# Two attention blocks backward: another order of the steps, an earlier last pair and refill at the block boundary, and x^T of the second block by a transposing DMA

## The chip, the cores and the metric

One core of one Trainium2 chip (the groups of runs were on different chips). The metric is the device time of one execution in microseconds, the median of several; every comparison below is with runs of the kernel before that were taken in the same rounds on the same chip. All runs used are in the fast state; the granted TensorE clock of the profiled ones is 0.993 to 0.998.

## The reference

Forward and gradients of two independent attention blocks with cached K and V. For each block B = 8 batches of 96 queries, D = 640, H = 32 heads of 128, 512 keys, all bf16:

```python
def _A_ref(x, k_cache, v_cache, wq, wo):
    q = (x @ wq).reshape(B, Sq, H, Dh).transpose(0, 2, 1, 3)
    scores = jnp.einsum("bhqd,bhkd->bhqk", q, k_cache) * (Dh ** -0.5)
    p = softmax(scores)
    o = jnp.einsum("bhqk,bhkd->bhqd", p, v_cache)
    return o.transpose(0, 2, 1, 3).reshape(B, Sq, H * Dh) @ wo
# out = concatenate([A, B], -1); outputs: out and, by vjp with grad_out,
# dx, dk, dv, dwq, dwo of both blocks
```

## The kernel before

The kernel is one list of pieces of work sorted by (tick, slot) and emitted in that order. A tick, called **step** here, is one head and one batch, so a block has 256 steps and heads go in pairs (16 steps for a pair). Steps are counted below from the start of block 2: step 0 is its first, negative ones belong to block 1. Each piece has an offset from the start of its pair (`HK`) or of its step (`OFF`); within a step `SLOTS` gives the order. All DMAs are issued by one queue, the sync engine's, in that same order.

```python
OFF = dict(kt=-3, vt=2, vn=1, kn=4, dv=7, dk=10, s2=3, s3=3, s4=4, s5=5, s6=6, s7=8, s8=9)
HK = [   # first and second head of a pair: loads, wo^T/wq^T, Q, dO, their transposes, O and dQ back, dwo, dwq
    dict(pA=-10, pB=-7, pC0=[-6, -4], pC1=[-5, -3], pD1=-2, pD0=0, qA0=21, qA1=25, qB=[28, 25]),
    dict(pA=-7, pB=-2, pC0=[-1, 1], pC1=[0, 2], pD1=3, pD0=6, qA0=29, qA1=33, qB=[36, 33], qD=[...]),
]
HK2 = [dict(HK[0], qA0=29, qB=[32, 31]), dict(HK[1], qA0=33)]      # first pair of block 2
GT0, ST0, ST1, NG0, NX0 = 2, -14, 7, 21, 26
SLOTS = dict(LOAD=0, S2A=5, S2B=5.5, S8=10, S7=20, S5=30, S4=40, S6=50, ...)
# S2: S and softmax; S8: dQ, dS^T; S7: dK; S5: O, P^T; S4: dV; S6: dP, delta, dS

# boundary, block 2: x and g are staged in three "ob" buffers and transposed on TensorE
for i in range(2 * TT):
    em.add(tick0 + ST0 + (ST1 * i) // (2 * TT), SL_LOAD + 0.5, setup_stage(i // TT, i % TT))
    em.add(tick0 + ST0 + (ST1 * i) // (2 * TT) + 2, SL_SETUP, setup_T(i // TT, i % TT))
for t in range(TT):    # refill of the single g_nat and x_nat, which the last pair of block 1 still reads
    em.add(tick0 + NG0 + t, SL_LOAD + 0.5, setup_nat(1, t, t + 1))
    em.add(tick0 + NX0 + (3 * t) // 2, SL_LOAD + 0.5, setup_nat(0, t, t + 1))
# ...
def qB(h, di):         # dwo of one head, in two pieces (columns 0:512 and 512:640)
    if "dwo_sb" not in st:
        st["dwo_sb"] = hd.tile([128, D], BF16, name="dwo_sb", bufs=1)
    # ... 6 matmuls into w_ps, then evac() by ScalarE into dwo_sb
# ...
for di in range(len(dsplits)):
    em.add(c0t + hk["qB"][min(di, len(hk["qB"]) - 1)], SL_HEAD + 1, qB(h, di))
em.add(c0t + max(hk["qB"]) + 2, SL_LOAD + 0.3, qB_st(h))      # the store, two steps later
```

Other single or scarce buffers that matter: `dK_sb` has three, `V_sb`, `K_sb` and `VT_p` four, `KT_p` five, and all PSUM tiles share eight banks. A second `dwo_sb` takes 1.25 KB more in each partition of SBUF; the experiments pay for it with a `KT_p` buffer, as the author found no room otherwise (no run here shows that).

## Time and profile before

| | before |
|---|---|
| median of 4 runs | 1669.48 us (1669.2 to 1673.67) |
| profiled span, granted clock | 1668.0 us, 0.993 |
| busy: TensorE, VectorE, ScalarE, GpSimd | 97%, 82%, 80%, 32% |
| TensorE busy in a slice of 41.7 us: steady / at the boundary | 41.4 to 41.7 in most (three of block 1: 38.6, 40.5, 40.9) / 31.6 to 41.1 |

Read the slices, not the average: a steady slice of TensorE is full, so only what takes columns off its stream or fills its few holes can change the time. The prediction shows the lines.

### The profile page before, as it was taken

To read this page: it belongs to the slowest core of one execution; us is meant where nothing else is said; L and a number is where in the kernel's file an instruction comes from. 1 tells how busy PE (TensorE), PEld (TensorE's weight loads), DVE (VectorE), ACT (ScalarE), POOL (GpSimd) and SP (SyncE) were. 2 spreads that over 40 slices of the span, in tenths; PEclk is the share of its full clock that TensorE was granted. 3 is DMA by queue.
4 is the path that set the end of the run, shared out by engine and by line. 5 is a ranking of instruction groups with operands and counts; after the bars stand their busy time and mean duration, and the time that the engine had idled before them with its cause. 6 is when DMAs were issued, how large, how long until landed. Compare 5 with 4: busy or idle time off the path is not lost.

```text
span 1668.0 us, 55517 instructions
## 1 busy us (share of the span) xinstructions
PE 1616.8 (97%) x20920; PEld 1265.7 (76%) x20920; DVE 1368.3 (82%) x3389; ACT 1339.2 (80%) x3517; POOL 533.5 (32%) x1030
## 2 busy tenths in 40 slices
PE   7999999999999999998998799999999999999998
PEld 5777877777777777877777678777787777878776
DVE  5887888888888888887887678888888888888886
ACT  6989877779788788886877699778797887878783
POOL 2333333333333333332333233333333333333331
PEclk9999999999999999999999899999999999999999
DMA  9999999999999999999999999999999999999995
GB/s 253 265 280 270 279 283 270 267 282 273 291 271 287 278 280 279 298 257 271 274 295 282 284 252 281 289 279 267 282 297 286 275 266 276 288 273 270 281 281 173
DMA packets 372430, 458.13 MB, mean 275 GB/s; under 512 B 36800, under 2 KB 363968, under 8 KB 363968
## 3 DMA queue, kind: packets, MB, share of 16 engines
q1 hardware_dynamic: 372160, 454.57, 102.7%
q8 instruction: 164, 2.69, 0.7%
q14 instruction: 106, 0.87, 0.1%
HBM read 161.09 MB, written 159.12 MB: 192 GB/s over the span
## 4 chain that ended last, share of the span: by engine, by line
PE 79%; ACT 6%; DMA 6%; DVE 5%; issue 2%; SPq 1%; POOL 0%; ACTq 0%; DVEq 0%
PE q_ps L239 11%; PE o_ps L524 10%; PE dwo_ps L479 6%; PE dV_ps L375 5%; PE dP_ps L399 5%; PE dwq_ps L499 5%; PE S_ps L303 5%; PE dK_ps L441 5%; PE optp_ps L350 4%; PE optp_ps L357 4%; PE dq_dst_ps L418 4%; PE dq_dst_ps L425 4%; PE n_ps L254 3%; PE nat_ps L465 2%; DVE negm L305 2%
## 5 line engine op out<-in xcount | busy, mean ns | idle before, releaser
L334 POOL TENSOR_SCALAR P_sb<-E_sb,rinv 96x512 bf16<-96x512 bf16 x512 | 352.7, 689 | 297.4 <-DVE rinv L325 296.8
L389 POOL TENSOR_TENSOR prod<-OT_h,dOT_h 128x96 bf16<-128x96 bf16 x512 | 186.8, 365 | 806.0 <-DVE OT_h L361 757.6
L446 ACT ACTIVATE dK_sb<-dK_ps 128x512 bf16<-128x512 f32 x512 | 304.4, 594 | 166.2 <-PE dK_ps L441 159.9
L315 ACT ACTIVATE E_sb<-S_ps,negm 96x512 bf16<-96x512 f32 x512 | 349.4, 682 | 74.3 <-DVE negm L305 68.8
L403 DVE SCALAR_TENSOR_TENSOR dS_sb<-dP_ps,dl_ps,P_sb 96x512 bf16<-96x512 f32 x512 | 382.4, 747 | 24.4 <-PE dl_ps L401 13.6
L305 DVE TENSOR_REDUCE negm<-S_ps 96x1 f32<-96x512 f32 x512 | 346.8, 677 | 57.1 <-PE S_ps L303 56.5
L380 ACT ACTIVATE dV_sb<-dV_ps 128x512 bf16<-128x512 f32 x512 | 309.7, 605 | 0.3 <-PE dV_ps L375 0.3
L364 ACT ACTIVATE PT_sb<-optp_ps 128x384 bf16<-128x384 bf16 x512 | 252.7, 493 | 5.0 <-DVE OT_h L361 4.2
L375 PE MATMUL dV_ps<-dOnat_h,P_sb 96*128 96x128 bf16 x2048 | 199.2, 220 | 0.0
L441 PE MATMUL dK_ps<-Qnat_h,dS_sb 96*128 96x128 bf16 x2048 | 198.6, 220 | 0.0
L427 DVE COPY dST_sb<-dq_dst_ps 128x384 bf16<-128x384 bf16 x512 | 177.6, 347 | 25.0 <-PE dq_dst_ps L425 20.2
L399 PE MATMUL dP_ps<-VT_p,dOT_h 128*96 128x512 bf16 x512 | 196.2, 383 | 0.0
L303 PE MATMUL S_ps<-KT_p,QT_h 128*96 128x512 bf16 x512 | 194.7, 380 | 1.5 <-ACT E_sb L315 0.4
L350 PE MATMUL optp_ps<-PT_sb,V_sb 128*128 128x96 bf16 x2048 | 172.4, 206 | 18.7 <-ACT dwo_sb L162 9.8
L357 PE MATMUL optp_ps<-ident,P_sb 96*128 96x96 bf16 x2048 | 172.6, 206 | 4.9 <-POOL P_sb L334 4.4
L418 PE MATMUL dq_dst_ps<-dST_sb,K_sb 128*128 128x96 bf16 x2048 | 171.4, 207 | 1.4 <-DVE dST_sb L427 1.1
L418 PEld LDWEIGHTS <-K_sb 128*128 128x128 bf16 x2048 | 133.3, 98 | 51.3 <-issue 2.9
L425 PE MATMUL dq_dst_ps<-ident,dS_sb 96*128 96x96 bf16 x2048 | 172.1, 205 | 0.0
L361 DVE CAST OT_h<-optp_ps 128x96 bf16<-128x96 f32 x512 | 126.6, 247 | 49.2 <-PE optp_ps L357 44.7
L524 PE MATMUL o_ps<-wo_r,OT_h 128*128 128x512 bf16 (+1 forms) x768 | 149.3, 299 | 0.0
L524 PE MATMUL o_ps<-wqT_h,dQT_h 128*128 128x512 bf16 (+1 forms) x768 | 148.5, 299 | 0.0
L350 PEld LDWEIGHTS <-V_sb 128*128 128x128 bf16 x2048 | 125.2, 97 | 23.0 <-issue 18.2
(71 smaller groups left out, 3064.4 us busy)
## 6 DMA issues: line engine op xcount, KB each, us to landing
out_dram<-dV_sb SPq DMA_DIRECT2D x256, 256.0 KB, 4.7
out_dram<-dK_sb SPq DMA_DIRECT2D x256, 256.0 KB, 4.6
V_sb<-in_A_v_cache_dram SPq DMA_DIRECT2D x128, 256.0 KB, 4.4
K_sb<-in_A_k_cache_dram SPq DMA_DIRECT2D x128, 256.0 KB, 4.5
V_sb<-in_B_v_cache_dram SPq DMA_DIRECT2D x128, 256.0 KB, 4.5
K_sb<-in_B_k_cache_dram SPq DMA_DIRECT2D x128, 256.0 KB, 4.4
out_dram<-dwo_sb SPq DMA_DIRECT2D x64, 160.0 KB, 4.6
out_dram<-dwq_sb SPq DMA_DIRECT2D x32, 320.0 KB, 4.7
```

The lines of the kernel that those rows point to most:

```text
L305: nc.vector.tensor_reduce(negm[:], S_ps[:], axis=AX.X, op=ALU.max, negate=True)
L315: nc.scalar.activation(E_sb[:].rearrange("q (a f) -> q a f", f=F4), st["S_ps"][:].rearrange("q (f a) -> q a f", f=F4), ACT.Exp, bias=st["n ...
L334: nc.gpsimd.tensor_scalar(P_sb[:], st["E_sb"][:], st["rinv"][:], 0.0, op0=ALU.mult, op1=ALU.add)
L350: nc.tensor.matmul(OT_ps, st["V_sb"][:, c, :], st["PT_sb"][:, c * Sq:(c + 1) * Sq], start=(c == 0), stop=(c == KC - 1))
L375: nc.tensor.matmul(dV_ps[:, c * 128:(c + 1) * 128], P_sb[:, c * 128:(c + 1) * 128], hs["dOnat_h"][:, b * 128:(b + 1) * 128], start=True, s ...
L380: nc.scalar.activation(dV_p[:, j], dV_ps[:], ACT.Identity, scale=1.0)
L399: nc.tensor.matmul(dP_ps[:], hs["dOT_h"][:, tok], st["VT"], start=True, stop=True)
L403: nc.vector.scalar_tensor_tensor(dS_sb[:].rearrange("q (a f) -> q a f", f=F4), dP_ps[:].rearrange("q (f a) -> q a f", f=F4), dl_ps[:, 0:1] ...
L418: nc.tensor.matmul(dQT_ps, st["K_sb"][:, c, :], st["dST_sb"][:, c * Sq:(c + 1) * Sq], start=(c == 0), stop=(c == KC - 1))
L441: nc.tensor.matmul(dK_ps[:, c * 128:(c + 1) * 128], dS_sb[:, c * 128:(c + 1) * 128], hs["Qnat_h"][:, b * 128:(b + 1) * 128], start=True, s ...
L446: nc.scalar.activation(dK_p[:, j], dK_ps[:], ACT.Identity, scale=1.0)
L524: nc.tensor.matmul(o_ps[:], src[:, t * 128:(t + 1) * 128], rhs, start=(hh == 0), stop=(hh == groups[g] - 1))
```

## The change

Its intent, part by part: **(a)** x^T of block 2 comes by five transposing DMAs instead of thirty TensorE transposes, g is staged four steps ahead, and the heads of block 2's first pair move with it; **(b)** the last pair of block 1 does its dwo and dwq sooner (`HKE`), so that the refills of g and x can start at step 15 and spread to step 28, and block 2's first pair does its dwo sooner; **(c)** wq and wo are loaded two steps sooner; **(d)** at the start g and the first wo are loaded two steps sooner; **(e)** inside a step TensorE does dK, dQ and dS^T, dP, O and P^T, dV. The diff, cut to its core:

```diff
-    dict(pA=-10, pB=-7, ...),
+    dict(pA=-12, pB=-7, ...),
-HK2 = [dict(HK[0], qA0=29, qB=[32, 31]), dict(HK[1], qA0=33)]
-GT0, ST0, ST1, NG0, NX0 = 2, -14, 7, 21, 26
+HK2 = [dict(HK[0], pB=-5, pC0=[-6, -4], pC1=[-1, 0], pD1=1, pD0=2, qB=[28, 27]), dict(HK[1], pC0=[-2, 0], pC1=[1, 2])]
+HKE = [dict(HK[0], qB=[23, 22]), dict(HK[1], qA0=25, qA1=27, qB=[29, 28], qD=[(30, 0, 2), (31, 2, 4), (32, 4, 5)])]
+GT0, NG0, NX0 = 0, 15, 18
-SLOTS = dict(..., S8=10, S7=20, S5=30, S4=40, S6=50, ...)
+SLOTS = dict(..., S7=10, S8=20, S6=25, S5=30, S4=40, ...)
+            sp(nc.sync.dma_start_transpose(S["xT"][:, c, :], x_flat[:, c * 128:(c + 1) * 128]))
-        for i in range(2 * TT):    # staging and TensorE transposes of x and g
-            ...
+        for c in range(DC):
+            em.add(tick0 - 14 + c, SL_LOAD + 0.5, setup_xT(c))
+        for t in range(TT):
+            tt = tick0 - 8 + 5 * (t // 3)
+            em.add(tt - 4, SL_LOAD + 0.5, setup_stage(t))
+            em.add(tt, SL_HEAD - 1, setup_T(1, t))
-            em.add(tick0 + NX0 + (3 * t) // 2, SL_LOAD + 0.5, setup_nat(0, t, t + 1))
+            em.add(tick0 + NX0 + 2 * t, SL_LOAD + 0.6, setup_nat(0, t, t + 1))
-            hk = (HK if h >= HP else HK1 if first else HK2)[j]
+            hk = (HKE if first and h >= H - HP else HK if h >= HP else HK1 if first else HK2)[j]
+            soon = 2 if first and HP <= h < 2 * HP and j == 0 else 0    # pair 1 keeps its load steps
```

More of the change, by code (lines that the diff above doesn't have):

```diff
@@ L46 @@
 HK = [
-    dict(pA=-10, pB=-7, pC0=[-6, -4], pC1=[-5, -3], pD1=-2, pD0=0, qA0=21, qA1=25, qB=[28, 25]),
+    dict(pA=-12, pB=-7, pC0=[-6, -4], pC1=[-5, -3], pD1=-2, pD0=0, qA0=21, qA1=25, qB=[28, 25]),
     dict(pA=-7, pB=-2, pC0=[-1, 1], pC1=[0, 2], pD1=3, pD0=6, qA0=29, qA1=33, qB=[36, 33], qD=[(37, 0, 2), (38, 2, 4), (39, 4, 5)]),
@@ L57 @@
 GSPREAD1 = 9
-SLOTS = dict(LOAD=0, S2A=5, S2B=5.5, S8=10, S7=20, S5=30, S4=40, S6=50, S3A=52, S3B=53, S5B=54, HEAD=SL_HEAD, GRP=SL_GRP)
+SLOTS = dict(LOAD=0, S2A=5, S2B=5.5, S7=10, S8=20, S6=25, S5=30, S4=40, S3A=52, S3B=53, S5B=54, HEAD=SL_HEAD, GRP=SL_GRP)
 class Chain:
@@ L134, in setup_nat, with setup_stage, setup_xT, f @@
         return f
-    def setup_stage(which_, t):
+    def setup_stage(t):
         def f():
-            key, _, src_flat = KEYS[which_]
-            S[(key, t)] = wk.tile([128, D], BF16, name="ob", bufs=3)
-            sp(nc.sync.dma_start(S[(key, t)][:], src_flat[t * 128:(t + 1) * 128, :]))
+            S[("g_nat", t)] = wk.tile([128, D], BF16, name="ob", bufs=3)
+            sp(nc.sync.dma_start(S[("g_nat", t)][:], g_flat[t * 128:(t + 1) * 128, :]))
+        return f
+    def setup_xT(c):
+        def f():
+            if c == 0:
+                S["xT"] = const.tile([128, DC, T], BF16, name="xT", bufs=1)
+            sp(nc.sync.dma_start_transpose(S["xT"][:, c, :], x_flat[:, c * 128:(c + 1) * 128]))
         return f
@@ L176, in build_block @@
     else:
-        for i in range(2 * TT):
-            em.add(tick0 + ST0 + (ST1 * i) // (2 * TT), SL_LOAD + 0.5, setup_stage(i // TT, i % TT))
-            em.add(tick0 + ST0 + (ST1 * i) // (2 * TT) + 2, SL_SETUP, setup_T(i // TT, i % TT))
+        for c in range(DC):
[4 more added lines that the diff above has]
+            em.add(tt, SL_HEAD - 1, setup_T(1, t))
         for t in range(TT):
             em.add(tick0 + NG0 + t, SL_LOAD + 0.5, setup_nat(1, t, t + 1))
-            em.add(tick0 + NX0 + (3 * t) // 2, SL_LOAD + 0.5, setup_nat(0, t, t + 1))
+            em.add(tick0 + NX0 + 2 * t, SL_LOAD + 0.6, setup_nat(0, t, t + 1))
     def pA_wq(h):
@@ L551, in build_block @@
             c0t = tick0 + (h - j) * B
-            hk = (HK if h >= HP else HK1 if first else HK2)[j]
+            hk = (HKE if first and h >= H - HP else HK if h >= HP else HK1 if first else HK2)[j]
             early = first and h < HP
+            soon = 2 if first and HP <= h < 2 * HP and j == 0 else 0
             if j == 0:
-                em.add(tick0 - 15 if early else c0t + hk["pA"], SL_LOAD + (1 if early else 0), pA_wq(h))
-            em.add(tick0 + GT0 if early else c0t + hk["pA"], SL_LOAD - 1 if early else SL_LOAD, pA(h))
+                em.add(tick0 - 15 if early else c0t + hk["pA"] + soon, SL_LOAD + (1 if early else 0), pA_wq(h))
+            em.add(tick0 + GT0 if early else c0t + hk["pA"] + soon, SL_LOAD - 1 if early else SL_LOAD, pA(h))
             em.add(c0t + hk["pB"], SL_HEAD, pB(h))
```

## The prediction

> **What bounds the kernel now.** I read first the page's busy shares, then the stretches table (the span in 40 equal slices, busy time of each engine), then the table of waits, then the timeline around the largest waits. The page:
>
> ```profile
> PE 1616.8 (97%) x20920; PEld 1265.7 (76%) x20920; DVE 1368.3 (82%) x3389; ACT 1339.2 (80%) x3517; POOL 533.5 (32%) x1030
> PE 79%; ACT 6%; DMA 6%; DVE 5%; issue 2%; SPq 1%; POOL 0%; ACTq 0%; DVEq 0%
> ```
>
> TensorE is busy 97% and is 79% of the chain that ended last. A busy TensorE need not run at its rate, so I checked in the timeline that it streams: from the first dP matmul of a step to the next instruction there are 0.22 us for 512 columns, and four 128-column dK matmuls take 0.22 to 0.23 us. Away from the ends and the block boundary the slices look like the first row below; only a few do not (columns: PE, PEld, DVE, ACT, POOL busy us with counts, granted clock, DMA share, GB/s).
>
> ```profile
> 417.00:458.70 41.70, 41.55 (x524) 31.86 (x523) 34.93 (x88) 32.12 (x84) 12.51 (x25) 1.00 1.05 291
> 750.60:792.30 41.70, 37.09 (x470) 29.40 (x468) 30.14 (x75) 27.52 (x70) 10.62 (x21) 0.96 1.00 271
> 834.00:875.70 41.70, 40.16 (x507) 30.35 (x506) 33.55 (x87) 32.66 (x88) 12.87 (x25) 1.00 1.07 295
> 875.70:917.40 41.70, 37.33 (x470) 29.24 (x469) 32.18 (x81) 30.70 (x81) 12.94 (x25) 0.96 1.03 282
> 917.40:959.10 41.70, 31.56 (x405) 25.40 (x402) 25.11 (x60) 25.53 (x70) 9.94 (x20) 0.88 1.02 284
> ```
>
> So the steady state is bound by the TensorE stream itself and the idle time sits in 750 to 960 us, where block 1 hands over to block 2 (plus 14 us in the first two slices and 5 in the last). What TensorE waits for there, from the table of its waits:
>
> ```profile
> PE optp_ps L350 <- ACT dwo_sb L162: 9.8, 1, 9.8
> PE woT_ps L209 <- DMA wo_r<-in_A_wo_dram: 4.8, 4, 2.2
> PE optp_ps L350 <- DMA V_sb<-in_B_v_cache_dram: 4.2, 2, 2.6
> PE tp_ps L151 <- DMA ob<-in_grad_out_dram: 3.3, 2, 2.8
> PE tp_ps L151 <- DMA ob<-in_B_x_dram: 1.8, 2, 1.5
> ```
>
> The 9.8 us is one wait. ScalarE's timeline shows it: nothing runs on it from 927.7 to 937.8, as it stands at the write of dwo_sb of head 1 (second row) behind the store of head 0 out of the same single buffer.
>
> ```profile
> 927.25 0.49 ACT L364 ACTIVATE PT_sb<-optp_ps 128x384 bf16<-128x384 bf16 x1
> 937.79 0.28 ACT L162 ACTIVATE dwo_sb<-dwo_ps 128x128 bf16<-128x128 f32 x1 [10.05 <-DMA out_dram<-dwo_sb]
> ```
>
> The sync queue's timeline says why the store was late: it issues at 933.31 and lands at 937.7, and the queue had been issuing back to back since 906 because the x and g refills stood in it among the K and V loads:
>
> ```profile
> 926.59 0.46 SPq L133 DMA_DIRECT2D x_nat<-in_B_x_dram  x1
> 927.10 1.23 SPq L266 DMA_TRANSPOSE KT_p<-in_B_k_cache_dram  x1
> 929.95 0.47 SPq L133 DMA_DIRECT2D x_nat<-in_B_x_dram  x1
> 933.31 0.46 SPq L485 DMA_DIRECT2D out_dram<-dwo_sb  x1
> ```
>
> **What the Trainium skill says.** "TensorE: Matmul & The Clock Gate", section "Wait — 56ns, not 53.3ns?", gives columns over 2.4 GHz plus about 2.5 ns from start to start; the 0.22 us for 512 columns and for 4 x 128 columns agree. The same page, section "Part 1: The HAM clock gate", has the clock halve after an idle window of about 3.4 us; the slice with the 9.8 us wait has a granted clock of 0.88, the other two with waits 0.96, so it agrees, and a wait costs more than its length. The same page, "Architectural detail: the array is 16x 32x32, not 1x 128x128", calls ScalarE and VectorE strict FIFO; the empty ScalarE above agrees. "DMA: Bandwidth & Descriptors", section "DMA Transpose (X-bar)", allows transposing DMAs only from the sync and scalar queues, of 2-byte data, into SBUF; x is bf16 and all transposes stay on one queue, so no wait between streams is added. KT_p already comes this way (5.1 us to landing).
>
> **The change, part by part.** A step (the code's tick) is one head and batch: S_ps matmuls start 3.15 us apart on average. Per two steps the sync queue issues two transposing loads (1.1 to 1.2 us each), two plain loads (0.53), two stores (0.42), with about 0.1 between: near 4.7 of 6.3 us. So 1.6 us in two steps is left, room for three extra DMAs at 0.52.
>
> (a) x^T of block 2 by DMA. Gone: 30 transposes on TensorE, 30 x 0.056 = 1.7 us of stream, and 6 evictions off ScalarE and VectorE. g^T stays on TensorE but is staged four steps ahead, not two (12 us against a landing of 4.4), so the waits on "ob" (3.3 + 1.8) and the issue waits of the third staging buffer go. The slice at 750 lost 41.55 - 37.09 = 4.5 us of busy time and 0.04 x 41.7 = 1.7 us of clock, the next one 0.4: 6.6 us, all of it gone if the queue keeps up. Sum -8.3. Against: in steps -14 to -7 before block 2 the queue gets 5 transposes, 6 stagings and 6 of the usual extras, by my count 30.5 us against 25 of TensorE work; the loads run four steps ahead, less landing some 4 us of slack, so the excess of 5 costs about +1.5. Net -7.
>
> (b) The last pair of block 1 and the refills. The new qB order of block 2's first pair stores head 0 at step 30 and rewrites at 33; before, the rewrite (33) stood ahead of the store (34). That removes the 9.8 us for certain. The three slices from 834 lost 1.4 + 4.2 + 10.0 = 15.6 us of busy time; of their clock loss (1.7 + 5.0) about 3 lies outside the waits: 18.5 in all. But refills are not thinner, only earlier: g at 15 to 20, x at 18 to 28 (before 21 to 26 and 26 to 33), beside the twelve output stores at 8 to 26. With dwo and dwq moved ahead, steps 20 to 25 carry little TensorE work (about 2.4 us each by adding up their matmuls), and there I count 19.7 us of queue against 14.5. Summing from step 18 the queue falls some 7 us behind; before, the same count gave 5 and the waits on V_sb (4.2). With 4 us of slack I keep +4. Net -14.5.
>
> (c) wq, wo two steps earlier from pair 2 on: the late wo_r in the steady state, 1.1 us. Pair 1 keeps its time, so its wait (2.2) stays. Net -1.
>
> (d) g loads at step 0, not 2, with the first wo: one of the woT waits, 1.5 us, less a little for V later in the queue. Net -1.
>
> (e) Step order. No instruction is added. dK first gives dST one more 0.22 us before dQ reads it; dP before O gives P_sb 0.25 us more before P^T and starts VectorE's dS earlier. dl comes 0.55 us sooner after S, so prod has less time. All engines have the same work, and the steady slices have at most 0.2 us of visible idleness each, so it can earn only the rest: "optp_ps <- P_sb" 4.4 us (half at the two ends), "dwo_ps <- dK_sb" 2.4, 0.3 at the shortest step of each second pair. I take -3.
>
> Sum: -7 - 14.5 - 1 - 1 - 3 = -26.5, so 1669.7 - 26.5 = 1643 us, 1.6% less.
>
> **The rivals.** First, the queue lag replaces the wait (the likeliest). For it: the DMA share is 1.0 and over everywhere, landings come back to back from 885 to 937, and the light steps 20 to 25 lie exactly in the new refill. It would put V_sb waits of 8 to 10 us there and 3 to 5 at -8, where a wait over 3 us also halves the clock: 1652 to 1656. Against it: while TensorE waits the queue catches up, so loss cannot exceed its lag of 7. Second, the order creates a wait of its own: P_sb (0.69) and prod (0.37) share GpSimd, and in steps under 2.3 us (4 of 32) dl may stand waiting for prod, 0.3 us each: 512/32 x 4 x 0.3 = 19 us at worst, ending near 1662. Against it: GpSimd is 32% busy and from the end of O the chain of copy, dS and prod comes to about 1.6 us, under the shortest step of 1.8. Third, the order does more than I grant: S, dP and dV are spread more evenly over the eight banks, so head matmuls meet freed banks and the small gaps after dl and n_ps also go; with no lag at the boundary that is 1669.7 - 8.3 - 18.5 - 2 - 8 = 1633. Fourth, the transpose of x in 256-byte rows is much slower than that of KT and holds the queue; each 5 us of that shows as a wait on xT before q_ps, up to +10. No row of the profile has such a shape.
>
> **Range and chances.** The sure part is 9.8 + 5.1 + 1.7 = 16.6 us, giving 1653; the full sum of everything found is 1633. With order and lag each uncertain by some 6 us I say 1643, with 1630 to 1657. Over 2% faster means below 1636.3: that needs the third rival without the first, 0.23. Slower by 2% would need the order to cost 60 us: 0.01. Within 2%: 0.76.
>
> **What would show it.** Right: no tp_ps wait and no tp_ps matmul on x in block 2; no ScalarE gap on dwo_sb over 1 us; slices from 750 to 960 at 40 us busy or more and clock 1.00, except one near steps 20 to 26 with V_sb or VT_p waits of a few us; steady slices at 41.5. Wrong: TensorE waits for V_sb summing above 8 us (first rival), a dl_ps wait on prod recurring in every pair (second), TensorE idle under 20 us in all with the span below 1635 (third), q_ps waiting for xT (fourth).

## The result, and the profile after

1657.06 us median of 4 runs (1652.66 to 1658.7) against 1669.48: ratio 0.9916, 95% interval 0.989 to 0.9941. A ratio is the record's own, over all fast runs of the same rounds, so not quite the ratio of the medians quoted. Taken again later on another occasion the same kernel gave 1656.98 against 1664.51, ratio 0.9952 (0.9929 to 0.9976). So it is 0.5% to 0.8% faster, where 1.6% was predicted; 1657.06 lies at the upper end of the range of 1630 to 1657.

The page after, and the slices of the boundary with one steady one (columns as in the prediction; the line numbers of the code have moved by 7 to 10):

```profile
PE 1605.9 (97%) x20698; PEld 1263.3 (76%) x20890; DVE 1338.9 (81%) x3386; ACT 1349.3 (81%) x3514; POOL 534.9 (32%) x1030
PE 86%; DMA 5%; ACT 4%; issue 2%; DVE 2%; POOL 1%; SPq 1%; ACTq 0%; DVEq 0%
```

```profile
417.00:458.70 41.70, 41.30 (x520) 31.55 (x524) 34.45 (x88) 32.62 (x84) 12.56 (x24) 1.00 1.05 290
750.60:792.30 41.70, 37.74 (x482) 30.06 (x485) 31.96 (x80) 29.07 (x75) 11.54 (x22) 0.96 1.04 254
792.30:834.00 41.70, 35.25 (x453) 27.74 (x456) 29.13 (x72) 29.23 (x76) 11.46 (x22) 1.00 1.07 294
834.00:875.70 41.70, 37.98 (x430) 28.37 (x436) 27.35 (x69) 28.40 (x71) 10.49 (x20) 0.92 0.97 277
875.70:917.40 41.70, 40.78 (x554) 32.32 (x557) 37.31 (x96) 35.85 (x95) 14.56 (x28) 1.00 1.03 282
917.40:959.10 41.70, 39.15 (x498) 30.46 (x502) 30.61 (x76) 34.95 (x95) 13.52 (x26) 1.00 1.07 284
```

The hole of 917 to 959 us (31.56 busy before) has closed, and another has opened from 792 to 876. (About 190 of the 20,890 matmul records are missing in this trace, so a tenth or two less in a steady slice means nothing: the weight loads are all there.) TensorE's own waits name it:

```profile
PE dP_ps L409 <- ACT dwo_sb L169: 6.7, 1, 6.7
PE q_ps L249 <- ACT dwo_sb L169: 3.7, 3, 3.3
PE optp_ps L360 <- DMA V_sb<-in_B_v_cache_dram: 0.7, 1, 0.7
PE tp_ps L158 <- DMA ob<-in_grad_out_dram: 0.3, 1, 0.3
```

The waits for staged x and g (1.8 and 3.3 us) and for V_sb (4.2) that the prediction lists are gone or small, but ScalarE again stands behind a store of dwo_sb, in ScalarE's and the sync queue's timelines (rows between those shown are left out, here and below):

```profile
827.28 0.49 ACT L374 ACTIVATE PT_sb<-optp_ps 128x384 bf16<-128x384 bf16 x1
837.08 0.28 ACT L169 ACTIVATE dwo_sb<-dwo_ps 128x128 bf16<-128x128 f32 x1 [9.31 <-DMA out_dram<-dwo_sb]
```

```profile
824.89 0.57 SPq L198 DMA_DIRECT2D wq_p<-in_B_wq_dram  x1
833.42 0.46 SPq L495 DMA_DIRECT2D out_dram<-dwo_sb  x1
```

Which store is it? The load of wq belongs to step 4 (c0t = 16 and pA = -12), so the store at 833.42 is that of step 6. Head 29, the last one *not* in `HKE`, writes dwo at 36 after a pair start of -32, that is step 4, and stores at step 6. Head 30 writes from 22 after -16: also step 6. With a single buffer, ScalarE is to write in the very step in which the store of the old contents is only issued.

To see where time went, I took the start of the `negm` reduction (the row maximum for the softmax, one for each step) from each timeline, and compared how long stretches of steps lasted (us; each from one profiled execution, differences to before):

| steps | before lasts | after | order alone (e5) | x^T alone (e6) | last pair, refill alone (e7) | early loads alone (e11) | dwo later (e1) |
|---|---|---|---|---|---|---|---|
| -13 to -7 | 28.90 | -7.60 | -1.92 | -8.50 | -3.94 | -3.77 | -8.42 |
| -7 to 3 | 29.36 | +8.69 | -0.05 | +6.95 | +0.82 | +0.48 | +8.15 |
| 7 to 9 | 5.00 | +10.07 | -0.22 | 0.00 | +9.78 | 0.00 | -0.21 |
| 13 to 17 | 12.98 | +4.30 | -0.24 | +0.08 | +4.32 | 0.00 | +4.63 |
| 17 to 23 | 20.50 | -4.29 | -0.01 | +0.34 | -4.32 | +0.04 | -4.28 |
| 29 to 35 | 24.38 | -5.31 | -2.58 | -1.63 | -5.20 | -0.90 | -4.16 |
| 35 to 37 | 15.96 | -10.29 | -1.09 | +0.65 | -9.25 | -0.43 | -11.45 |
| 67 to 195 | 399.56 | -2.56 | -2.60 | -0.56 | -0.28 | -0.48 | -2.61 |

Rows repeat to hundredths where nothing waits for a DMA, which makes this a sharp tool. Where something does, they don't: the changed kernel taken again (e10) has -8.42, +6.76 and +8.81 in the first three rows, and e7, whose code is that of the kernel before up to step 6, has -3.94 in the first. So a difference of some 4 us in the first row shows nothing. Block 1's stretches are left out: they differ by up to 6.5 us between five profiles with the same code there (after, e1, e8, e9, e10). Two gains were taken back: 10.3 at steps 35 to 37 by 10.1 at 7 to 9, and 7.6 before step -7 by 8.7 after it. (13 to 17 and 17 to 23 only show work of the last pair that moved.)

### The profile page after: what moved, and what is told of

Its sections match the earlier page's. It is cut to its first block, busy times and chain, and to the rows that moved or that the text cites. A ratio compares the mean times of both kernels' runs of the same rounds, so it can differ in the third digit from the quotient of the medians.

```text
span 1656.3 us, 55400 instructions
## 1 busy us (share of the span) xinstructions
PE 1605.9 (97%) x20698; PEld 1263.3 (76%) x20890; DVE 1338.9 (81%) x3386; ACT 1349.3 (81%) x3514; POOL 534.9 (32%) x1030
## 4 chain that ended last, share of the span: by engine, by line
PE 86%; DMA 5%; ACT 4%; issue 2%; DVE 2%; POOL 1%; SPq 1%; ACTq 0%; DVEq 0%
PE o_ps L534 12%; PE q_ps L249 12%; PE dwq_ps L509 6%; PE dV_ps L385 6%; PE dK_ps L451 6%; PE S_ps L313 6%; PE dwo_ps L489 6%; PE dP_ps L409 6%; PE optp_ps L360 5%; PE optp_ps L367 5%; PE dq_dst_ps L428 5%; PE dq_dst_ps L435 5%; PE n_ps L264 3%; DMA out_dram<-dK_sb 2%; PE nat_ps L475 2%
## 5 line engine op out<-in xcount | busy, mean ns | idle before, releaser
L451 PEld LDWEIGHTS <-dS_sb 96*128 96x128 bf16 x2048 | 147.5, 97 | 48.4 <-issue 0.3
L360 PEld LDWEIGHTS <-V_sb 128*128 128x128 bf16 x2048 | 108.2, 96 | 55.1 <-issue 6.4
L534 PE MATMUL o_ps<-wo_r,OT_h 128*128 128x128 bf16 (+1 forms) x721 | 144.5, 294 | 2.4
L534 PE MATMUL o_ps<-wqT_h,dQT_h 128*128 128x128 bf16 (+1 forms) x721 | 144.3, 294 | 2.5
```

What stands on the lines that cost most here:

```text
L360: nc.tensor.matmul(OT_ps, st["V_sb"][:, c, :], st["PT_sb"][:, c * Sq:(c + 1) * Sq], start=(c == 0), stop=(c == KC - 1))
L451: nc.tensor.matmul(dK_ps[:, c * 128:(c + 1) * 128], dS_sb[:, c * 128:(c + 1) * 128], hs["Qnat_h"][:, b * 128:(b + 1) * 128], start=True, s ...
L534: nc.tensor.matmul(o_ps[:], src[:, t * 128:(t + 1) * 128], rhs, start=(hh == 0), stop=(hh == groups[g] - 1))
```

## The experiments

**Theory A**: the change moved the wait on the single dwo buffer from step 33 to step 6; the collision is one of the schedule and of a buffer, worth 10 us. **Rival B**: the DMA side is overrun at the boundary, and a wait taken away comes back elsewhere. For the parts: the predicted terms, each alone.

### e1: dwo of the last pair three steps later

```diff
-HKE = [dict(HK[0], qB=[23, 22]), dict(HK[1], qA0=25, qA1=27, qB=[29, 28], ...)]
-GT0, NG0, NX0 = 0, 15, 18
+HKE = [dict(HK[0], qB=[26, 25]), dict(HK[1], qA0=27, qA1=28, qB=[32, 31], ...)]
+GT0, NG0, NX0 = 0, 17, 18
```

> The changed kernel with only the last pair of block 1 rescheduled: dwo of its first head at steps 26 and 25 instead of 23 and 22, of its second at 32 and 31 instead of 29 and 28, g refill from step 17 instead of 15. The store of the head before it is issued at step 22, so the write to the single dwo buffer now comes three steps after that store and not in the same step. Theory A (the wait of 9.3 us on ScalarE and 6.7 us on TensorE near 830 us is a buffer collision made by the schedule, which costs about 10 us on the clock): that wait vanishes or shrinks below 2 us and the time is 1646 to 1650 us against 1657. Theory B (the sync queue is overrun at the block boundary and any wait removed there comes back as another, on V_sb, VT_p or dwo_sb): 1653 to 1658 us, with new waits of the same size within 60 us of the old one.

1647.51 us against 1667.06, ratio 0.9889 (0.9868 to 0.991). Steps 7 to 9 are 10.3 us shorter than in the changed kernel, some 5 of which come back later, between steps 9 and 43. ScalarE's waits in the table of waits:

```profile
ACT dK_sb L456 <- DMA out_dram<-dK_sb: 16.6, 11, 3.1
ACT dwo_sb L169 <- DMA out_dram<-dwo_sb: 14.2, 12, 2.5
```

The longest on dwo_sb is 2.5 us (before this edit 9.3), and the slice from 834 to 875.7 has TensorE busy for 41.70 of 41.70 us at clock 1.00. Theory A stands for this wait. Of rival B the 5 us that come back are a sign. The waits on dK stores, 8.7 us in 7 in the changed kernel and 16.6 in 11 here, are none: they spread as much without this edit (10.1 in 9 in e10, 14.7 in 10 in e3).

### e2 and e3: two buffers for dwo_sb, and the control

```diff
-name="dwo_sb", bufs=1)
+name="dwo_sb", bufs=2)        # e2 only
-bufs=5 if which == 0 else 4)  # KT_p, VT_p
+bufs=4)                       # e2 and e3: the room for it
```

> The changed kernel with two buffers for dwo_sb, paid for by four instead of five for KT_p (no room otherwise). Takes away every wait of ScalarE on a dwo store: in the profile of the changed kernel 21.5 us in 8 waits, the two large ones 9.3 and 4.3. Theory A: 1642 to 1648 us, since both large waits and the half clock after them go. Theory B (queue overrun): 1652 us or more, waits move to loads. If KT_p with four buffers costs something by itself, the control run beside it shows it.

> Control: the changed kernel with four buffers for KT_p and nothing else. Each theory expects the time of the changed kernel, 1655 to 1660 us, since the transposing loads of K run behind TensorE anyway and not ahead; if it is slower by more than 3 us, that is to be taken off the run with two dwo buffers.

e2: 1648.47, ratio 0.9882 (0.9859 to 0.9906). e3: 1654.57, ratio 0.9935 (0.9911 to 0.9958), so the fifth KT_p buffer is not missed by more than the noise here. Two buffers gain 0.5% over their control, some 8 us; steps 7 to 9 take 1.1 us more than before, in the control 9.2 more. 5.8 us of lateness then show up at steps 23 to 29, as rival B said in part.

### e4: two dwo buffers in the kernel before

The edit of e2 on the kernel before.

> The kernel before with two buffers for dwo_sb (and four for KT_p). Theory A: the 9.8 us wait of TensorE near 928 us goes, with the half clock after it: 1656 to 1660 us, as much as the whole change won, without any of it. Theory B: the waits on V_sb at that place grow instead and the time stays above 1664 us.

1656.86 us, ratio 0.9937 (0.9913 to 0.9961). One buffer in the old kernel gains about what the whole change gains. Steps 35 to 37 lose their 11.05 us, and nothing comes back within 30 steps (4.2 us do in steps 67 to 195, where this execution has a wait of 1.8 us on a load of wo with a spell of 3.4 us at half clock behind it). With a second buffer the 9.8 us wait is gone although the refills stay where they were; how long it would be with the refills elsewhere no run shows.

### e5: the order of the steps alone

```diff
-SLOTS = dict(..., S8=10, S7=20, S5=30, S4=40, S6=50, ...)
+SLOTS = dict(..., S7=10, S8=20, S6=25, S5=30, S4=40, ...)
```

> The kernel before with the new order of the steps alone. My prediction gave this part -3 us. Theory A (TensorE streams at its rate in the steady state, order moves waits of tenths): within 4 us of the kernel before, 1663 to 1668 us against 1667, the 9.8 us wait near 928 us still there; per 160 steps of block 2 the position of the steps differs by 1 to 3 us, as between the two full kernels. Theory C (the order frees banks sooner and is the main gain of the change): 1655 to 1660 us.

1660.71 against 1664.90, ratio 0.9971 (0.996 to 0.9983): 4.8 us faster, which falls between the theories (A said within 4 us); the 2.6 us in steps 67 to 195 are as A said. One place where it comes from, step 201, behind two short steps of its pair (2.35 and 2.65 us in the kernel before), in TensorE's timeline (start, length of the group), first before, then e5:

```profile
1456.53 0.34 PE L425 MATMUL dq_dst_ps<-ident,dS_sb 96*128 96x96 bf16 x4
1456.70 0.39 PE L441 MATMUL dK_ps<-Qnat_h,dS_sb 96*128 96x128 bf16 x4
1457.23 0.33 PE L350 MATMUL optp_ps<-PT_sb,V_sb 128*128 128x96 bf16 x4
```

```profile
1445.08 0.39 PE L441 MATMUL dK_ps<-Qnat_h,dS_sb 96*128 96x128 bf16 x4
1445.30 0.34 PE L418 MATMUL dq_dst_ps<-dST_sb,K_sb 128*128 128x96 bf16 x4
1445.65 0.38 PE L399 MATMUL dP_ps<-VT_p,dOT_h 128*96 128x512 bf16 x1
1445.94 0.20 PE L401 MATMUL dl_ps<-ones,prod 128*96 128x1 bf16 x1
1446.04 0.33 PE L350 MATMUL optp_ps<-PT_sb,V_sb 128*128 128x96 bf16 x4
```

Before, 0.53 us pass from dK to O, for a group that streams in 0.22: 0.31 us of standing still, once in every pair. In e5 dK goes on to dQ after 0.22 us and O comes later, with what it needs at hand. A smaller stop of about 0.15 us appears in its place: dl starts at 1445.94, when dP (1445.65 + 0.22) would have let it start at 1445.87, and O 0.10 after dl. By the medians of steps 77 to 236 five of the sixteen steps of a pair get 0.16 to 0.22 us shorter, others up to 0.15 longer, and a pair as a whole some 0.3 us shorter; no dl wait recurs with a size that would carry the second rival of the prediction.

### e6: x^T by DMA alone

The part (a) of the diff on the kernel before, with the heads of block 2's first pair that go with it, dwo of that pair as before.

> The kernel before with x^T of block 2 by transposing DMA, the earlier staging of g and the later heads of block 2's first pair that go with it; the order of the steps, the last pair and the refills as before. My prediction gave -7 us. Theory A (the five transposes and the stagings put the sync queue behind, which gives back in steps -7 to +3 what steps -13 to -7 win): -2 to +3 us against the kernel before, a gain of 7 us up to step -7 and a loss of 6 to 9 up to step +3. Theory D (the transposing DMA is as good as predicted, and what was given back came with other parts): -6 to -9 us.

1664.44 against 1664.90, ratio 1.0005 (0.9987 to 1.0022): nothing. The stretch table shows the two halves: -8.50 up to step -7, +6.95 up to step 3. What happens in the second half is a sync queue that has fallen behind. In the changed kernel's timeline of it, each transposing DMA of x takes 1.3 us to issue, as long as one of V:

```profile
775.71 0.52 SPq L287 DMA_DIRECT2D V_sb<-in_A_v_cache_dram  x1
776.33 0.41 SPq L296 DMA_DIRECT2D out_dram<-dV_sb  x1
776.79 1.31 SPq L147 DMA_TRANSPOSE xT<-in_B_x_dram  x1
778.20 1.26 SPq L276 DMA_TRANSPOSE VT_p<-in_A_v_cache_dram  x1
```

Counting V_sb loads (each belongs to a known step) against the S matmuls started by then, the queue of e6 is one step behind TensorE at -13 and -11, three at -9 and -7, two until 3; in the kernel before it is one behind up to -3 and two from -1 to 3. The stops then fall wherever a buffer is short; in e6 ScalarE's timeline has two on dK stores:

```profile
795.04 0.60 ACT L455 ACTIVATE dK_sb<-dK_ps 128x512 bf16<-128x512 f32 x1 [2.22 <-DMA out_dram<-dK_sb]
803.88 0.60 ACT L455 ACTIVATE dK_sb<-dK_ps 128x512 bf16<-128x512 f32 x1 [3.10 <-DMA out_dram<-dK_sb]
```

### e7: the last pair and the refills alone

The parts (b) of the diff on the kernel before (HKE, HK2's qA0 and qB, NG0, NX0).

> The kernel before with only the last pair of block 1 and the first of block 2 rescheduled and the g and x refills at their new steps. My prediction gave -14.5 us. Theory A (the collision on the single dwo buffer moves from step 33 to step 6 with the same 10 us): -4 to +2 us, a wait of ScalarE on a dwo store of 8 us or more near 840 us and none near 928. Theory D (the collision at step 6 comes of the queue lag that the transposes of x cause): no such wait, -10 us or better.

1662.83 against 1664.90, ratio 0.9990 (0.9979 to 1.0001). Theory A: the step 7 to 9 stretch is 9.78 us longer with no transposing DMA of x anywhere, and 35 to 37 is 9.25 shorter. ScalarE's timeline:

```profile
834.16 0.28 ACT L163 ACTIVATE dwo_sb<-dwo_ps 128x128 bf16<-128x128 f32 x1 [8.47 <-DMA out_dram<-dwo_sb]
```

### e8: the x refill later as well

```diff
-GT0, NG0, NX0 = 0, 17, 18     # on e1
+GT0, NG0, NX0 = 0, 17, 22
```

> The changed kernel with the last pair's dwo three steps later (as in the first run here, 1647.5 us) and in addition the x refill from step 22 to 32 instead of 18 to 28, since it is first needed at step 37. Theory B' (the refill's place in the queue costs what is left between steps 17 and 31, some 4 us): 1643 to 1646 us. Theory A (buffers made the waits, the lag costs little): no change, 1646 to 1650.

1649.73 us, ratio 0.9911 (0.989 to 0.9932): no gain on e1, of other rounds. My idea that the place of the x refill still costs 4 us was wrong.

### e9: the small boundary loads from GpSimd's queue

```diff
-            sp(nc.sync.dma_start(...))      # on e1: six stagings of g, six g and six x refills of block 2
+            nc.gpsimd.dma_start(...)
```

> The changed kernel with the last pair's dwo three steps later (the first run here), and the eighteen small loads of block 2 at the boundary (six stagings of g, six of the g refill, six of the x refill) issued from GpSimd's queue instead of the sync queue. Theory I (the sync queue's issue time, near 0.5 us for each DMA, in its one order is what falls behind): the waits of steps -7 to +3 and 17 to 31 shrink, 1640 to 1645 us. Theory T (the transfers themselves are at the limit, the share of the DMA engines is over 1.0 there, so it does not matter who issues): within 2 us of that first run's ratio, 0.987 to 0.991 of the kernel before. A loss of over 3 us would mean that GpSimd's own issuing delays P_sb and prod.

1650.51 us, ratio 0.9907 (0.9878 to 0.9937), against 0.9889 for e1. Who issues these loads makes no difference, and steps -7 to 3 are still 8.7 us longer than before (+2.82 up to step -3, +5.92 after it). The Trainium skill says as much in "DMA: Bandwidth & Descriptors", section "Issuing engines are not separate DMA queues": DMAs of all engines run on the same 16 DMA engines, and issuing from several saves only the sequencer's time. This run agrees. The transposes of x themselves stayed on the sync queue.

### e10: the changed kernel again

No edit; for the chip of e9 and e11.

> The changed kernel unaltered, to have it on the same chip as the others of this call and to see how its executions spread. Ratio near the first result, 0.989 to 0.994, for each theory.

1656.98, ratio 0.9952 (0.9929 to 0.9976); a little above what was expected; its executions spread from 1648.7 to 1661.2. Its steps 7 to 9 again take 8.81 us more than before.

### e11: the earlier loads alone

```diff
-    dict(pA=-10, ...)
+    dict(pA=-12, ...)            # with soon = 2 for pair 1 of block 1
-GT0, ... = 2, ...
+GT0, ... = 0, ...
```

> The kernel before with only the earlier loads: g and the first wo at step 0 instead of 2, wq and wo two steps earlier from the third pair on. My prediction gave -2 us for the two. Theory A: -1 to -3 us, waits on wo_r (4.8 us in the profile of before) at least halved. A rival: nothing, because the load that comes sooner delays V and K behind it in the same queue.

1659.0 against 1664.51, ratio 0.9965 (0.9952 to 0.9978): 5.8 us faster, more than any theory expected; with e5 the part that gains (the two intervals overlap). The waits of TensorE on wo_r, 4.8 us in the profile of before (7.0 in e5, 6.4 in e7), are gone from its table. The rest of the 5.8 us is not placed: most of it must lie in block 1, where these loads are and where single executions differ too much.

### e12: a fourth dK_sb buffer

```diff
-name="dK_sb", bufs=3)                 # on e1
+name="dK_sb", bufs=4)
-bufs=5 if which == 0 else 4)
+bufs=4)
```

> The changed kernel with the last pair's dwo three steps later (the first run here, ratio 0.989), and a fourth buffer for dK_sb, paid for by four instead of five for KT_p. It takes away what makes ScalarE wait for dK stores: 16.6 us in 11 waits in that run, one of 3.1 us near 800 us, where the transposes of x have put the sync queue some three steps behind. Theory A (the lag hurts through the output buffers that are short, so each buffer added is a gain): 3 to 6 us less than that run, ratio 0.985 to 0.987. Theory T (the lag is of the transfers, and what one buffer lets through stops at VT_p, V_sb or the staging of g next): ratio 0.988 to 0.991, the stretch from step -7 to +3 still 6 us or more longer than before.

1654.25 us, ratio 0.9936 (0.991 to 0.9961): no gain, rather worse than e1. ScalarE's waits on dK stores went from the table of waits; TensorE got others in their place:

```profile
PE optp_ps L360 <- DMA V_sb<-in_A_v_cache_dram: 7.5, 10, 1.9
PE optp_ps L360 <- ACT dwo_sb L169: 3.5, 4, 1.3
```

Ten waits on V_sb in block 1, where e1 has none. The control e3, which has four KT_p buffers too, shows the same wait, shorter:

```profile
PE optp_ps L360 <- DMA V_sb<-in_A_v_cache_dram: 3.7, 4, 1.7
```

But e6, with five, has three of these waits as well (3.6 us), so how much of them KT_p's missing buffer makes stays open. Steps -7 to 3 still cost +5.55 us, as in e3 with three dK_sb (+5.59): the fourth gave nothing there. In the one execution profiled the loss against e1 lies before step -13 (5.2 us longer than before, e1 0.3 shorter).

The best are e1 and e2, equal within the noise: 1.1% to 1.2% faster than the kernel before. e1 is 0.3% to 0.6% ahead of the changed kernel by the two ratios taken of that, of other rounds, and 0.5% ahead of e3 in the same rounds.

## Why the prediction was half right

The parts measured alone, with 1665 us for the kernel before of those rounds, beside the predicted terms:

| part | predicted us | measured us | by |
|---|---|---|---|
| (a) x^T by DMA | -7 | +0.8 | e6, 1.0005 |
| (b) last pair, refills | -14.5 | -1.7 | e7, 0.9990 |
| (c), (d) earlier loads | -2 | -5.8 | e11, 0.9965 |
| (e) order | -3 | -4.8 | e5, 0.9971 |
| sum | -26.5 | -11.5 | whole: -8.0 and -14.0 by its two ratios |

The parts add up to the whole within its own spread, so no interaction of the parts is shown. That 1657 came so near the range was luck: (a) and (b) gave 20.6 us less than predicted, and (c) to (e) 5.6 more.

- **What bounds the kernel** was right. The chain is TensorE for 86% after, steady slices stay full, and the gains that were placed came from holes. Two readings were off. The waits on wo_r (4.8 us) are listed among those of the hand-over, but all lie in block 1. And three slices of block 1 that miss 0.8 to 3.1 us of TensorE are passed over.
- **The clock**: the prediction says that the trace agrees with the idle window of about 3.4 us that it cites from the Trainium skill, and lets waits over 3 us halve the clock. The kernel before does show clock 0.50 from 770.6 to 774.0, from 907.1 to 910.5 and from 931.0 to 941.2. But the waits just before the first two lasted 1.5 and 2.6 us, and a wait of 2.8 us at 786 was followed by clock 1.00. So here a wait shorter than that window could end in half clock.
- **(b) failed at one step**: "That removes the 9.8 us for certain." It did at step 33. But I checked the order of store and rewrite for heads 0 and 1 of block 2 and, in the last pair, only for its two heads among themselves. The pair before it keeps its old steps, so the store of head 29 (step 6) meets the write of head 30 (step 6). e7 shows the +9.78 us without the rest of the change, e1 removes it with three steps, e2 against e3 removes it with a second buffer (1.1 us against 9.2), and e4 removes the old one so. The +4 for queue lag was the wrong term to hedge with: after the change TensorE waits for V_sb in block 2 for 0.7 us.
- **(a) failed by size, on both sides.** The -8.3 was read from one execution (-8.50 in steps -13 to -7 in e6 against it). Against e7, whose code is the same there, the gain is 4.6 us, or 6.7 with the 16 steps ahead of them, where e7 is 2.15 longer than before. On the other side stands the term "+1.5" for the excess in the queue. The excess of 5 us that I counted for steps -14 to -7 was near what came, but I let most of it vanish in the slack of loads running four steps ahead. Measured give-back: +6.95 (e6), +5.6 to +10.2 in the runs with the rest of the change. The lag was paid in full. Why the slack did not cover it stays open: that the shortest buffer sets it (dwo_sb one, dK_sb three) is my argument, and e12 with a fourth dK_sb does not bear it out.
- **(c) and (d)**: right in kind (wo_r waits gone), too small by 4 us; not traced further.
- **(e)**: right in kind and near in size. The stop of 0.3 us that it names is there, once in every pair and not in each second one. No wait of dl on prod of the second rival's size appeared.
- **The rivals**: the first one (the lag replaces the wait, 1652 to 1656 us) was nearest, though not through V_sb and less than the dwo collision. The second and fourth did not happen. x in 256-byte rows comes as fast as K (in the changed kernel xT lands after 5.0 us, KT_p after 5.1). Of the third (the order does more) e5 shows a part: 4.8 us for the 3 predicted.

**Open**: whether the lag after x^T is the queue's issue time (5 x 1.3 us) or the transfers. e9 shows that issuing the small loads elsewhere gains nothing, which speaks for the transfers, but a run with the five transposes themselves off the sync queue was not made.

## What to carry to other kernels

When pieces of a schedule are moved for one pair or one tile, check every reuse of a single buffer across the seam to the neighbour that was *not* moved: the store must be issued, and land, before the next write, and behind an in-order ScalarE one such collision costs the whole store path. Don't let a lag of the queue vanish in the loads' lead: here it was paid in full. Take a stretch that waits for DMAs from more than one execution before you count its waits as gain. And measure the parts of a combined change alone: here the two small terms gave most of the gain and the two large ones cancelled themselves.

## What the Trainium skill lacked or had wrong

- "TensorE: Matmul & The Clock Gate", section "Back-to-back issue gap": gives 81 ns a matmul of 128 columns and 131 ns for 512 as the sustained rate of LDWEIGHTS and MATMUL pairs. Here four 128-column matmuls, each with its own weights, take 0.22 us (55 ns each), and one of 512 columns 0.22 us. The page's formula for an isolated gap fits instead.
- "DMA: Bandwidth & Descriptors" has no issue time in us of a DMA on trn2's sync queue (only sequencer cycles of "previous generations", in a comparison with trn3). Here: transposing loads 1.1 to 1.3 us where they are short (the profile has them up to 4.2 us, which may hold waits), plain loads 0.4 to 0.6, stores 0.42, and about 0.1 between. With 1788 DMAs in 1668 us in the kernel before, this is a budget of its own.
- No page has the cost of rewriting a single store buffer too early: the place of the store in the queue plus 4.6 us to landing, the longest such wait of ScalarE is 8.1 to 10.1 us in the eight profiles here that keep the collision.
